# A linear-attention block gated by a mixer MLP: one more pair of feature chunks of the last block in seven products, one unused split less, and a new order

## The chip, the core and the metric

The kernel runs on one core of a Trainium2 chip. The metric is the device time of one execution in microseconds. The core has five engines that each work through a list of their own, in order: PE (TensorE, matrix products), DVE (VectorE), ACT (ScalarE), POOL (GpSimd) and SP (SyncE). In this kernel SP issues the plain transfers, and POOL issues the transfers that add to what stands at their destination. Engines wait for each other by semaphores only.

## The reference

The input `x` has 2048 tokens of 512 features. It is layer-normed, goes through a linear attention with 32 heads of 16 features, and the result is multiplied by a gate: a SiLU of a mixer block with an MLP of 1376 features.

```python
def _A_ref(x, wqkv, wo):
    q, k, v = ...                                  # x @ wqkv, 32 heads of 16
    phi = lambda t: jnp.where(t > 0, t + 1, jnp.exp(t)) + 1e-6
    pq, pk = phi(q), phi(k)
    kv = jnp.einsum("bhsd,bhse->bhde", pk, v)
    o = num / den                                  # pq @ kv over pq . sum(pk)
    return o @ wo
def _B_ref(x, w1, w2, w3, w4):
    h = _gelu(_layernorm(x) @ w1)
    x1 = x + shifted_by_quarters(h) @ w2           # shifts of +1, -1, +2, -2 tokens
    return x1 + _gelu(_layernorm(x1) @ w3) @ w4
xn = _layernorm(x)
return x + _A_ref(xn, ...) * _silu(_B_ref(xn, ...))
```

## The kernel before, in words

Tokens are worked in four blocks of 512 (four tiles of 128 each). Every fp32 operand of a product is split into a rounded high part and the rest (`halves`, `rounded`, `split`: one ACT or DVE copy and one DVE subtraction), and a product is three matmuls: high x high, low x high, high x low (`products`, L514). All matmuls are issued from L151.

First come keys, queries and the sums over tokens (`key`, `keys_queries`, `gram`) together with the first half of the mixer (`mix1`, tiles `h`; `mix2`, tiles `pam`, `pbm`, `pem`). Its weight `w1` is centred first: four chunks of `w1` are added by a load and three adding transfers of POOL into `w1t`, summed over rows by PE (`w1m`), scaled by ACT, and added to the four raw chunks `w_s` by four more transfers of POOL. Then the sums over tokens, `v`'s weight and `wo` are folded into one 512 x 512 matrix `M`, held as quarters `b11`, `b12`, `b21`, `b22` and four combinations `t1` to `t4`, each split in two.

Then the MLP runs block by block. Its 1376 features are 11 chunks of at most 128: five pairs (chunk s with chunk s + 5) and a last one of 96. `up_pair` (L1293) or `up_plain` (L1270) make a pair's hidden features; both take seven products of halves in place of eight (`seven`, L948, Strassen's scheme in Winograd's form). What comes back down is taken by `downs` (L1360) in one of two ways. For a pair whose number is below `SEVENS[b]` of its block, the down product is also made of seven products: `up_pair` forms four sums and differences of the hidden quarters (`s1` to `s4`), `make_t4` (L1183) or the memory `w4t` gives those of `w4` (`t1` to `t4`), five products stream into the accumulators (`STREAM`), and the other two (`s2 t2`, `s3 t3`) are done for all such pairs at the last of them, in `chain` (L1386), through the bank `uc`. For the other pairs and the last chunk, `plain` (L1353) makes the products of each token tile directly. `SEVENS` (L464) holds the number for each block.

The attention is done for two tiles at a time (`attend_pair`, tiles `pas`, `pbs`, `pes`, result `so`), and `gate` (L1481) finishes a token tile: it adds the accumulator to `e` (what `chain` and the residual left there), takes SiLU on ACT (`th`), multiplies by `so` on DVE, adds `x`, and stores. In the last block tiles 2 and 3 have `x` loaded ahead (`xr`, a DVE addition); tiles 0 and 1 add it by a transfer of POOL from memory (`pl.gather(th, x[rows])`), and the store follows it. The last half of tile 3 has its accumulator in the bank `a4x`, into which the residual `xi` goes by two matmuls. In the last block the down products of the last `keep` groups are left for the end, token tile by token tile (L1683 and the loop over `rest`).

The code doesn't run in the order in which it is written. Each operation is recorded, and `Plan.emit` (L296) lays the recorded list out in time with its own durations for every operation: of those that are ready on an engine it takes the one with the earliest due time. Due times come from a matmul's place in the written order, passed back to what it needs. `nudged` (L253) changes the due time of single operations by a table, `SOONER`: pairs of an operation's number and a step of a quarter microsecond by which it is due sooner (or later, with a minus). What comes out is one fixed list for each engine.

Of the kernel before, what the change touches and what calls it, by code (L numbers as in the profile page):

```python
# [27 lines left out]
class Tile:  # L28
# [16 lines left out]
    @property  # L45
    def all(self):
        return self[:, :]
# [383 lines left out]
def linear_attn_gated_by_mixer(  # L431
# [29 lines left out]
    EARLY = (), ()  # L461
    QAT, SAT = ((2, 3),) * 4, ((4, 5),) * 4
    HURRY = 3.0
    SEVENS = 0, 2, 3, 3  # L464
    FIRST7 = 1
    SUMS = "DVE"
    LATE = QT
# [16 lines left out]
    def piece(name, dt=F32):  # L484
        return pl.new("p", name, dt, PIECE)[:, :512]

    def rounds(name):

        return piece(name + "h", F32R), piece(name + "l", F32R)
# [13 lines left out]
    def both(pair, a, z):  # L503

        return tuple(v.cols(a, z) for v in pair)

    def in2(v, n=TH):

        return v.via(lambda ap: ap.rearrange("p (c n) -> p c n", n=n))
# [12 lines left out]
    def rounded(hi, lo, full, src=None):  # L522

        pl.act(hi, src or full, AF.Copy)
        split(lo, full, hi)

    def halves(name, src):

        hi, lo = rounds(name)
        rounded(in2(hi), in2(lo), src)  # L530
        return [both((hi, lo), c * TH, (c + 1) * TH) for c in range(2)]
# [688 lines left out]
    def load_group(b, s):  # L1220
# [4 lines left out]
        if s == "last":  # L1225
            load_w4(b, FB - 1)
            return
        if s >= SEVENS[b]:
            for f in (s, s + NS):
                load_w4(b, f)  # L1230
            return
        if all(s >= n for n in SEVENS[:b]):
            make_t4(b, s)
# [59 lines left out]
    def up_pair(b, s):  # L1293

        if s >= SEVENS[b]:
            up_plain(b, s)
# [63 lines left out]
    def downs(b, acc, s, which=range(QT)):  # L1360
        fs = (FB - 1,) if s == "last" else (s, s + NS)
        if b < FIRST7:
            for f in fs:
                for j in range(QT):
                    down(b, f, j, acc[j].all)
        elif s != "last" and s < SEVENS[b]:
            if s < SEVENS[b] - 1:
                stream(b, acc, s)
# [17 lines left out]
    def chain(b, n):  # L1386
# [3 lines left out]
        t, e = UC[b][0][0].tile, EV[b]  # L1390
        for s in range(SEVENS[b]) if n else ():
            x, y = CHAIN[n]
# [42 lines left out]
    def forms_m():  # L1435
        tf = [piece(f"m_f{k}") for k in range(4)]
        ts = right([in2(MQ[h][d]) for h in range(2) for d in range(2)], lambda k: in2(tf[k]))
        for k, v in enumerate(ts):
            M[f"t{k + 1}"] = halves(f"m_t{k + 1}", v)

# [22 lines left out]
    def attend_pair(i):  # L1463
# [3 lines left out]
        z = [o1.cols(0, TH), o1.cols(TH, 512), o2.cols(TH, 512), o2.cols(0, TH)]  # L1467
        ps = seven(f"s{i}", z, lambda x, y: [QF[i][x][c] + M[y][c] for c in range(2)])
        pl.act(z[3], ps, AF.Copy)
# [149 lines left out]
    b = NQ - 1  # L1619
# [24 lines left out]
    MQ = [[piece(f"mq{h}{d}") for d in range(2)] for h in range(2)]  # L1644
# [11 lines left out]
    for gg in range(NC):  # L1656
        ps = bank(f"m{gg}")
        products(ps, [both(kvs, gg * P, (gg + 1) * P) + wos[gg]])
        for d in range(2):
            pl.act(MQ[gg // 2][d].cols(gg % 2 * TH, (gg % 2 + 1) * TH), ps.cols(d * TH, (d + 1) * TH), AF.Copy)  # L1660
    M = {f"b{h + 1}{d + 1}": halves(f"m_b{h + 1}{d + 1}", in2(MQ[h][d])) for h in range(2) for d in range(2)}
    turn_y(0)
    load_last()
    load_group(0, "last")
# [1 line left out]
    for b in range(NQ):  # L1666
        last = b == NQ - 1
        acc = [pl.new("acc", f"acc{b}_{j}", F32, 512) for j in range(QT)] if b < FIRST7 else {}
        if b >= FIRST7:
            t = [pl.new("acc", f"a{j}_{b}", F32, 512) for j in range(QT)]  # L1670
            side = [[half(v, d) for d in range(2)] for v in t]
            if last:
                side[QT - 1][1] = half(pl.new("mm", "a4x", F32, 512), 0)
            for k, (h, d) in QUARTER.items():
                acc[k] = [(side[2 * h + j][d], d == 0 or last and h == j == 1) for j in range(2)]
            acc["rows"] = [[(v.all, 0, 512)] for v in t]
            if last:
                acc["rows"][QT - 1] = [(side[QT - 1][d], d * TH, (d + 1) * TH) for d in range(2)]
            t = pl.new("mm", f"uc{b}", F32, 512)
            acc["a1"] = UC[b] = [(half(t, j), j == 0) for j in range(2)]  # L1680
        n7 = SEVENS[b]
        groups = list(range(n7)) + ["last"] + list(range(n7, NS))
        keep = 3 if last else 2  # L1683
        for n, s in enumerate(groups):
            if b == 0 and 0 < n < NS:
                load_pair(n)
            if n < NS:
                load_group(b, groups[n + 1])
            elif not last:
                load_group(b + 1, 0 if SEVENS[b + 1] else "last")  # L1690
            if s == "last":
                up_last(b)
            else:
                up_pair(b, s)
            if b == 0 and n == 1:
                forms_m()
            if n > 0:
                for k in range(2):
                    if n == QAT[b][k]:
                        for j in range(2):  # L1700
                            turn_q(b * QT + 2 * k + j)
                        forms_q(b * QT + 2 * k)
            if n > 0 and n - 1 < len(groups) - keep:
                downs(b, acc, groups[n - 1])
            for k in range(2):
                if n == SAT[b][k]:
                    attend_pair(b * QT + 2 * k)
        rest = groups[len(groups) - keep:]

        if b < FIRST7:  # L1710
            turn_y(b + 1)
            for s in rest:
                downs(b, acc, s)
            for j in range(QT):
                gate_tile(b, j, acc[j].all)
        elif not last:
            turn_y(b + 1)
            for s in rest:
                downs(b, acc, s)
            for j in range(QT):  # L1720
                gate(b, j, acc["rows"][j][0][0])
        else:
            xr = {}
            for j in (2, 3):
                xr[j] = piece(f"xr{j}")
                pl.load(xr[j], x[(b * QT + j) * P:(b * QT + j + 1) * P, :])
            t = piece("xi", F32R)
            hi, lo = t.cols(0, TH), t.cols(TH, 512)
            rounded(hi, lo, EV[b][QT - 1].cols(TH, 512))
            pl.patience = 0.0  # L1730
            for j in range(QT - 1):
                for s in rest:
                    downs(b, acc, s, (j,))
                gate(b, j, acc["rows"][j][0][0], xr=xr.get(j))
            for r, a, z in acc["rows"][QT - 1]:
                if a:
                    for v in (hi, lo):
                        pl.mm(r, identr.all, v, False, False, more=True)
                for s in rest:
                    for f in (FB - 1,) if s == "last" else (s, s + NS):  # L1740
                        ah, al, n = H3[b, f]
                        left = both((ah.rows(n), al.rows(n)), (QT - 1) * P, QT * P)
                        products(r, [left + both(W4[b, f], a, z)], False, more=True)
                gate(b, QT - 1, r, a, TH, xr=xr[QT - 1], whole=a > 0)

    SOONER = (
# [16 lines left out]
    )  # L1763
    pl.emit(first=6.0, lead={"p": 14.0, "w": 14.0}, reserve={"p": 20, "w": 1}, window=12.0,
            ahead=6.0, table=SOONER)
# [37 lines left out]
```

## Time and profile before

| | |
|---|---|
| median of 3 runs | 502.06 us (501.93 to 503.35) |
| profiled execution, first to last instruction (span) | 501.2 us, 0.9 us under the median |
| PE | 494.3 us busy (99%), 3102 matmuls |
| DVE, ACT, POOL | 440.9 us (88%), 388.9 us (78%), 84.9 us (17%) |
| granted TensorE clock | 1.000 |

The profile's own span runs from the first to the last instruction of one execution; the run's time also holds what lies around it. A matmul of 512 columns stands with about 0.39 us in the list, and the next one starts 0.23 us after it: the records overlap, so that a busy PE says that work stood there, and the distance from start to start says how fast it went.

### The profile page before, as it was taken

The numbers are of one execution on the slowest core, as the hardware profiler recorded it, in microseconds if no ns is written. First come the engines' busy times: TensorE is split into PE (matmuls) and PEld (weight loads), VectorE is DVE, ScalarE is ACT, GpSimd is POOL, SyncE is SP. The second block draws the span as 40 slices with busy tenths as digits, with TensorE's granted clock in tenths as the row PEclk, the third lists the DMA queues.
The fourth block names the chain that finished last, engine by engine and source line by source line (L and its number), as shares of the span: only waits on it lengthen the run. The fifth ranks groups of instructions, "written<-read, shape, count | busy, mean of one in ns | idle before, by whom it ended". The sixth has DMA issues, their size and how long they took to land.

```text
span 501.2 us, 9464 instructions
## 1 busy us (share of the span) xinstructions
PE 494.3 (99%) x3102; PEld 442.2 (88%) x3102; DVE 440.9 (88%) x944; ACT 388.9 (78%) x859; POOL 84.9 (17%) x97
## 2 busy tenths in 40 slices
PE   8999999999999999999999999999999999999996
PEld 6777887898888888899999989999899998999986
DVE  5989999999699995999999998897799969998364
ACT  5999899867798884977777579957699878977551
POOL 1344433131221122020100002200020200201100
PEclk9999999999999999999999999999999999999999
DMA  7949985479994799979897599978699887898604
GB/s 245 365 110 239 319 261 144 106 149 269 322 260 134 191 336 233 262 198 286 266 319 243 193 312 260 269 235 245 190 252 305 225 192 239 278 314 266 154 8 120
DMA packets 86989, 116.69 MB, mean 233 GB/s; under 512 B 8864, under 2 KB 41148, under 8 KB 86940
## 3 DMA queue, kind: packets, MB, share of 16 engines
q1 hardware_dynamic: 77004, 98.00, 60.3%
q0 software_dynamic: 9936, 18.09, 20.9%
q8 instruction: 24, 0.39, 0.3%
q14 instruction: 25, 0.20, 0.2%
HBM read 73.70 MB, written 32.91 MB: 213 GB/s over the span
## 4 chain that ended last, share of the span: by engine, by line
PE 88%; DMA 8%; SPq 1%; ACT 1%; issue 0%; DVE 0%; POOL 0%; DVEq 0%
PE a L151 15%; PE pb L151 11%; PE h L151 9%; PE pbk L151 7%; PE g L151 7%; PE acc L151 6%; PE pe L151 6%; DMA w1t<-in_w 5%; PE pbm L151 5%; PE pbs L151 4%; PE uc L151 3%; PE pek L151 3%; PE pa L151 3%; PE pem L151 2%; PE pes L151 2%; PE pak L151 2%
## 5 line engine op out<-in xcount | busy, mean ns | idle before, releaser
L230 POOL DMA_DIRECT2D th<-in_x x14 | 12.3, 926 | 164.4 <-DMA w_t<-w4t 75.6
L230 POOL DMA_DIRECT2D o<-x x16 | 14.1, 895 | 65.1 <-DVE o L198 48.0
L178 ACT ACT_TABLE_LOAD x18 | 23.1, 1283 | 0.3
L652 POOL TENSOR_TENSOR rs<-w,nhalf 128x4 f32<-128x4 f32 (+2 forms) x10 | 16.7, 1675 | 38.1 <-DVE w L203 38.1
L173 ACT ACTIVATE gf<-gf 128x256 f32<-128x256 f32 (+1 forms) x48 | 22.0, 469 | 1.2 <-DVE gf L198 0.8
L230 POOL DMA_DIRECT2D zacc<-kr x16 | 16.4, 1022 | 36.5 <-DMA zacc<-kr 13.2
L230 POOL DMA_DIRECT2D e<-x1d x12 | 10.6, 1084 | 62.0 <-DVE e L198 44.1
L208 DVE SCALAR_TENSOR_TENSOR kr<-kt,kr 128x512 f32<-128x512 f32 x16 | 11.0, 686 | 4.4 <-ACT kt L173 4.4
L173 ACT ACT_TABLE_LOAD x11 | 14.1, 1283 | 1.0 <-PEq L1794 0.8
L173 ACT ACTIVATE ht<-ht 128x512 f32<-128x512 f32 x16 | 9.8, 623 | 6.5 <-DVE ht L198 6.5
L646 DVE BATCH_NORM_STATS2 st<-o 128x6 f32<-128x512 f32 x16 | 10.6, 681 | 4.7 <-DMA o<-x 4.7
L198 DVE TENSOR_TENSOR e<-a,e 128x512 f32<-128x512 f32 (+1 forms) x17 | 9.7, 587 | 5.1 <-PE a L151 5.1
L198 DVE TENSOR_TENSOR th<-th,so 128x512 f32<-128x512 f32 (+1 forms) x17 | 10.9, 648 | 3.3 <-ACT th L173 3.3
L173 ACT ACTIVATE x<-x,nm,rs 128x512 f32<-128x512 f32 x16 | 12.9, 805 | 0.0
L173 ACT ACTIVATE p<-pe 128x256 f32<-128x256 f32 x20 | 7.6, 382 | 6.7 <-PE pe L151 6.5
L173 ACT ACTIVATE p<-pb 128x256 f32<-128x256 f32 x20 | 7.6, 381 | 6.7 <-PE pb L151 6.5
L173 ACT ACTIVATE y<-o,nm,rs 128x512 f32<-128x512 f32 x16 | 11.8, 804 | 1.2 <-DVE nm L208 1.2
L173 ACT ACTIVATE th<-e 128x512 f32<-128x512 f32 (+1 forms) x12 | 7.1, 608 | 7.1 <-DVE e L198 7.1
L208 DVE SCALAR_TENSOR_TENSOR pq<-pq,qr 128x512 f32<-128x512 f32 x12 | 8.2, 686 | 3.9 <-ACT pq L173 3.8
L198 DVE TENSOR_TENSOR ht<-h,abc 128x512 f32<-128x512 f32 x16 | 10.8, 681 | 0.4 <-PE h L151 0.4
L198 DVE TENSOR_TENSOR gf<-pb,p 128x256 f32<-128x256 f32 x20 | 8.4, 418 | 3.1 <-PE pb L151 3.0
L208 DVE SCALAR_TENSOR_TENSOR qz<-pq,zb 128x512 f32<-128x512 f32 x16 | 10.7, 684 | 0.2
(1868 smaller groups left out, 2285.1 us busy)
## 6 DMA issues: line engine op xcount, KB each, us to landing
w_s<-in_w SPq DMA_DIRECT2D x34, 256.0 KB, 4.8
w_t<-w4t SPq DMA_DIRECT2D x26, 256.0 KB, 4.5
w_b<-w4d SPq DMA_DIRECT2D x24, 256.0 KB, 5.3
x<-in_x SPq DMA_DIRECT2D x16, 256.0 KB, 6.3
zacc<-kr POOLq DMA_DIRECT2D x16, 256.0 KB, 4.8
o<-x POOLq DMA_DIRECT2D x16, 256.0 KB, 4.7
x1d<-o SPq DMA_DIRECT2D x16, 256.0 KB, 3.8
xt<-in_xt SPq DMA_DIRECT2D x15, 256.0 KB, 6.2
```

What stands on the lines that cost most here:

```text
L151: lambda: nc.tensor.matmul(out.get(), lhs.get(), rhs.get(), start=start, stop=stop, skip_group_check=more))
L173: nc.scalar.activation(out.get(), src.get(), func, scale=get(scale), **kw)
L178: op.warm = lambda: nc.scalar.activation(self.scr[1].get(), self.scr[0].get(), func)
L198: self.vec(eng, out, [a, b], lambda: self.e(eng).tensor_tensor(out.get(), a.get(), b.get(), op=op), True)
L208: lambda: self.nc.vector.scalar_tensor_tensor(out.get(), a.get(), get(s), b.get(), op0=op0, op1=op1),
L230: lambda: self.nc.gpsimd.dma_start(out.get(), get(src), accum_op=ALU.add))
L646: pl.add("DVE", .62, .69, [xv], [st], lambda: nc.vector.bn_stats(st.get(), xv.get()))
L652: lambda: g.tensor_tensor(out.get(), src.get(), nh.get(), op=ALU.pow))
```

## The change

Three edits:

- `SEVENS` is `0, 2, 3, 4` in place of `0, 2, 3, 3`: in the last block pair 3 (chunks 3 and 8) takes seven down products too. `chain` now comes at pair 3, and `keep` is 2 for all blocks: the last chunk and pair 4 are left for the end, where the last chunk and the pairs 3 and 4 were.
- The quarter `b12` of the matrix `M` is no longer split into high and low part. None of the seven products uses it by itself.
- The table `SOONER` has another content: 1831 pairs in place of 163.

```diff
-    SEVENS = 0, 2, 3, 3
+    SEVENS = 0, 2, 3, 4
...
-    M = {f"b{h + 1}{d + 1}": halves(f"m_b{h + 1}{d + 1}", in2(MQ[h][d])) for h in range(2) for d in range(2)}
+    M = {f"b{h + 1}{d + 1}": halves(f"m_b{h + 1}{d + 1}", in2(MQ[h][d])) for h, d in ((0, 0), (1, 0), (1, 1))}
...
-        keep = 3 if last else 2
+        keep = 2
...
     SOONER = (
-        2, 309, 19, 38290, 23, 20, 24, 16, 26, 2469, 31, 130, 36, 38310, 42, 1201, 43, 154, 54, 5, 55, 36, 62, 32,
...
+        0, 800, 1, 227, 2, -732, 3, -637, 4, 627, 5, 416, 6, 55, 7, 1378, 8, -4, 9, -7, 10, 21, 11, -267, 12, -499,
...
+        5403, 22,
     )
```

The table moves instructions on every engine, from the first load to the last store. Three places follow; a row is line, operation, output tile, input tiles and size, with buffer numbers at the names' ends, and rows of an engine are executed in this order.

PE, the first block's mixer products `h`, from the first use of `w1`'s chunk 1 (`w_1h`) to the first use of chunk 2 (`w_2h`). Before, where six products with chunk 0 stand ahead of these rows:

```order
L151 MATMUL h_0_622<-u_1h,w_1h 128x512
L151 MATMUL h_0_622<-u_1l,w_1h 128x512
L151 MATMUL h_2_627<-u_1h,w_1h 128x512
L151 MATMUL h_0_622<-u_1h,w_1l 128x512
L151 MATMUL h_2_627<-u_1l,w_1h 128x512
L151 MATMUL h_2_627<-u_1h,w_1l 128x512
L151 MATMUL h_1_657<-u_0h,w_0h 128x512
L151 MATMUL h_1_657<-u_0l,w_0h 128x512
L151 MATMUL h_1_657<-u_0h,w_0l 128x512
L151 MATMUL h_1_657<-u_1h,w_1h 128x512
L151 MATMUL h_0_622<-u_2h,w_2h 128x512
```

Now, where eight products with chunk 0 stand ahead of these rows:

```order
L151 MATMUL h_0_634<-u_1h,w_1h 128x512
L151 MATMUL h_0_634<-u_1l,w_1h 128x512
L151 MATMUL h_1_647<-u_0h,w_0l 128x512
L151 MATMUL h_1_647<-u_1h,w_1h 128x512
L151 MATMUL h_0_634<-u_1h,w_1l 128x512
L151 MATMUL h_0_634<-u_2h,w_2h 128x512
```

The first use of chunk 2 was the 17th of these products and is the 14th.

PE, the third block's mixer: products of the token sums (`g`), of the mixer's first half (`h`) and the first of its second half (`pbm`, from the split hidden tile `ha112h`). Before:

```order
L151 MATMUL h_1_1935<-u_2h,w_2l 128x512
L151 MATMUL h_1_1935<-u_3h,w_3h 128x512
L151 MATMUL h_1_1935<-u_3l,w_3h 128x512
L151 MATMUL h_1_1935<-u_3h,w_3l 128x512
L151 MATMUL g_401<-k9l,x9h 128x512
L151 MATMUL g_401<-k9h,x9l 128x512
L151 MATMUL g_410<-k9h,x9h 128x512
L151 MATMUL g_410<-k9l,x9h 128x512
L151 MATMUL g_410<-k9h,x9l 128x512
L151 MATMUL pbm_2085<-w_b11h,ha112h 128x256
L151 MATMUL pbm_2085<-w_b11l,ha112h 128x256
```

Now:

```order
L151 MATMUL h_3_2033<-u_2h,w_2l 128x512
L151 MATMUL h_3_2033<-u_3h,w_3h 128x512
L151 MATMUL h_3_2033<-u_3l,w_3h 128x512
L151 MATMUL pbm_2071<-w_b11h,ha112h 128x256
L151 MATMUL h_3_2033<-u_3h,w_3l 128x512
L151 MATMUL g_369<-k8h,x8l 128x512
L151 MATMUL g_369<-k9h,x9h 128x512
```

The first `pbm` product stood after all `h` products of the block, with its fellows behind it; now it stands alone, ahead of the last `h` product.

The end of PE's list. `a_3` are the accumulators of the last block, `a4x` the one of the second half of tile 3, `pes` a bank of the attention of tiles 2 and 3. Before:

```order
L151 MATMUL a4x<-w_3_8h,f_8h 128x256
L151 MATMUL a4x<-w_3_8l,f_8h 128x256
L151 MATMUL a4x<-w_3_8h,f_8l 128x256
L151 MATMUL a4x<-w_3_4h,f_4h 128x256
L151 MATMUL a4x<-w_3_4l,f_4h 128x256
L151 MATMUL a4x<-w_3_4h,f_4l 128x256
L151 MATMUL a4x<-w_3_9h,f_9h 128x256
L151 MATMUL a4x<-w_3_9l,f_9h 128x256
L151 MATMUL a4x<-w_3_9h,f_9l 128x256
```

Now:

```order
L151 MATMUL a_3_6446<-w_3_9l,f_9h 128x512
L151 MATMUL a_3_6446<-w_3_9h,f_9l 128x512
L151 MATMUL a_3_6391<-w_3_4h,f_4l 128x512
L151 MATMUL a_3_6391<-w_3_9h,f_9h 128x512
L151 MATMUL a_3_6391<-w_3_9l,f_9h 128x512
L151 MATMUL a_3_6391<-w_3_9h,f_9l 128x512
L151 MATMUL pes_7122<-m_b22h,q14s1h 128x256
L151 MATMUL pes_7122<-m_b22l,q14s1h 128x256
L151 MATMUL pes_7122<-m_b22h,q14s1l 128x256
L151 MATMUL pes_7122<-m_b22h,q14s1h 128x256
L151 MATMUL pes_7122<-m_b22l,q14s1h 128x256
L151 MATMUL pes_7122<-m_b22h,q14s1l 128x256
```

And the end of DVE's list, the additions `e` and multiplications `th` of the last four token tiles. Before:

```order
L198 TENSOR_TENSOR e_6782<-a_3_6357,e_6782 128x512
L198 TENSOR_TENSOR th_0_7122<-th_0_7122,so_7080 128x512
L198 TENSOR_TENSOR e_6786<-a_3_6402,e_6786 128x256
L198 TENSOR_TENSOR th_0_7122<-th_0_7122,xr_6835 128x512
L198 TENSOR_TENSOR th_0_7142<-th_0_7142,so_7089 128x256
L198 TENSOR_TENSOR th_0_7142<-th_0_7142,xr_6857 128x256
L198 TENSOR_TENSOR th_256_7158<-th_256_7158,so_7089 128x256
L198 TENSOR_TENSOR th_256_7158<-th_256_7158,xr_6857 128x256
```

Now (`e_6774` and `th_0_7206` are tile 0, `e_6765` and `th_0_7188` tile 1, `th_0_7174` tile 2, `th_0_7155` half of tile 3):

```order
L198 TENSOR_TENSOR e_6765<-a_3_6446,e_6765 128x512
L198 TENSOR_TENSOR th_0_7155<-th_0_7155,so_7138 128x256
L198 TENSOR_TENSOR e_6774<-a_3_6391,e_6774 128x512
L198 TENSOR_TENSOR th_0_7188<-th_0_7188,so_6985 128x512
L198 TENSOR_TENSOR so_7125<-u2s_7073,pes_7122 128x256
L198 TENSOR_TENSOR th_0_7155<-th_0_7155,xr_6848 128x256
L198 TENSOR_TENSOR th_0_7174<-th_0_7174,so_7125 128x512
L198 TENSOR_TENSOR th_0_7174<-th_0_7174,xr_6837 128x512
L198 TENSOR_TENSOR th_0_7206<-th_0_7206,so_6949 128x512
```

The list ended with tile 3, whose `x` is in `xr`; it now ends with tile 0, whose `x` comes by a transfer of POOL. POOL's last two transfers are these additions of `x` in both kernels, for tiles 0 and 1 (`th_0_7048`, `th_0_7066` before, `th_0_7188`, `th_0_7206` now). SP's last stores were those of tiles 0, 1, 2 and the two halves of 3, and are now those of the halves of 3, then 2, 1 and 0.

193 rows, old and new, of the table SOONER are left out of this document.

## The prediction

> **What bounds the kernel now.** I read the page, then who PE waits for, then the start and the end in order of time. The page (busy time by engine, and the chain that ended last):
>
> ```profile
> span 501.2 us, 9464 instructions
> PE 494.3 (99%) x3102; PEld 442.2 (88%) x3102; DVE 440.9 (88%) x944; ACT 388.9 (78%) x859; POOL 84.9 (17%) x97
> PE 88%; DMA 8%; SPq 1%; ACT 1%; issue 0%; DVE 0%; POOL 0%; DVEq 0%
> ```
>
> All waits of PE in the whole execution (who for whom: us in total, times, longest):
>
> ```profile
> PE warm L151 <- POOL ones L548: 1.7, 1, 1.7
> PE w1m L151 <- ACT w1mh L173: 0.6, 1, 0.6
> PE h L151 <- ACT w_1h L173: 0.2, 1, 0.2
> ```
>
> So PE is the bound from the first product to its last matmul; behind the warm-up it waits 0.8 us by name. Time can change in three ways: fewer matmul columns, holes between matmuls, and what comes after the last matmul. Holes that no wait names show as wider steps (us, then busy and count by engine, clock, DMA share, GB/s):
>
> ```profile
> 5.50:12.00 6.50, 6.46 (x21) 4.27 (x22) 6.06 (x11) 3.81 (x7) 0.00 (x0) 1.00 1.01 314
> 32.10:46.00 13.90, 13.06 (x56) 9.65 (x56) 12.42 (x25) 12.97 (x36) 6.38 (x8) 1.00 0.81 173
> ```
>
> With the steps of 0.2325 us shown next, 21 wide matmuls take 4.9 of the first 6.5 us (1.6 lost), and of the second row's 56 (two are the narrow `ab` ones, hardly 0.03 us each) 12.6 of 13.9 us are used (1.3 lost). That is most of what PE can win back.
>
> **The change part by part: seven products.** The last matmuls of 512 and of 256 columns, first and last of five each:
>
> ```profile
> 491.83 0.40 PE L151 MATMUL a<-w_4l,f_4h 128*128 128x512 f32 x1
> 492.76 0.39 PE L151 MATMUL a<-w_9h,f_9l 128*128 128x512 f32 x1
> 496.20 0.28 PE L151 MATMUL a4x<-w_4l,f_4h 128*128 128x256 f32 x1
> 496.67 0.28 PE L151 MATMUL a4x<-w_9h,f_9l 128*128 128x256 f32 x1
> ```
>
> Four steps are 0.93 and 0.47 us: 0.2325 and 0.1175 us a matmul. Taken plainly, pair 3 costs 2 chunks x 3 tiles x 3 = 18 matmuls of 512 columns and, as tile 3 is done in halves, 12 of 256. In seven products it is 7 x 2 x 3 = 42 of 256. So 18 wide ones go and 30 narrow ones come: 30 x 0.1175 - 18 x 0.2325 = **-0.66 us**.
>
> The forms for it (DVE gets 12 more instructions, ACT 6, SP 7 transfers, with the two chunks of `w4` loaded again, four parts of `w4t` stored and read back) are made while PE works on the last block:
>
> ```profile
> 440.00:460.00 20.00, 20.00 (x171) 20.00 (x171) 16.96 (x40) 15.58 (x37) 0.86 (x1) 1.00 0.97 298
> 460.00:480.00 20.00, 20.00 (x162) 19.61 (x161) 10.45 (x24) 11.12 (x31) 3.51 (x4) 1.00 0.58 143
> ```
>
> Twelve DVE instructions of 0.42 to 0.69 us are at most 8 us; DVE is idle for 12.6 of these 40 us, ACT for 13.3. I take 0; without that cover PE stands still for what is late (a rival below). The split of `b12` that goes is one ACT and one DVE instruction where PE waits for neither: 0.
>
> **The order at the start.** The chunks of `w1` arrive by four POOL transfers:
>
> ```profile
> L230 POOL DMA_DIRECT2D w_s<-w1t x4: 909/1374/1894, 35.9 to 37.6; - x4
> DMA to landing us min/median/max: 3.4/6.4/8.6
> 44.80 0.49 PE L151 MATMUL h<-u_1h,w_1h 128*128 128x512 f32 x1 [0.22 <-ACT w_1h L173]
> 46.49 0.62 ACT L173 ACTIVATE w_2h<-w_s 128x512 fp32r<-128x512 f32 x1
> 46.55 0.39 PE L151 MATMUL h<-u_0l,w_0h 128*128 128x512 f32 x1
> 47.24 0.43 PE L151 MATMUL h<-u_2h,w_2h 128*128 128x512 f32 x1
> ```
>
> The last one, chunk 2, is issued at 37.6 and lands 8.6 us on, at 46.2; with its rounding on ACT (0.62) and two hand-overs of about 0.04 it can be used from 46.9. Before, its first use is the 17th `h` product, at 47.24, just not late. Now it is the 14th, and PE takes its list in order: the 14th product stood at 46.55 before (the row above) and can't start before 46.9 now. The two holes ahead of it, at `w1m` and `w_1h`, may close (their products stand later), but the wait for chunk 2 takes that back: **+0.35 us**. If all transfers of this chain come 1 us earlier, it is -0.65; 1 us later, +1.35.
>
> **The order in the middle.** Where `pbm` now stands alone, the first mixer tile must be ready 12 rows (2.8 us) after its last `h` product. Before:
>
> ```profile
> L173 ACT ACTIVATE ha112h<-ht x2: 400/408/417, 148.3 to 151.1; 128x256 fp32r<-128x256 f32 x2
> 154.78 0.28 PE L151 MATMUL pbm<-w_b11h,ha112h 128*128 128x256 f32 x1
> ```
>
> It was written at 151.5 and used at 154.78, 3.3 us later. Now DVE (0.69), GELU on ACT (0.63) and the rounding (0.41), with hand-overs about 2.0 us, must fit into 2.8: 0.8 us are left for what stands ahead on ACT, and two more 512-wide copies there (0.52 us a step) already make a hole. The new order strews single matmuls between other groups at many places, and behind the token sums only one narrow matmul instead of six covers the copy for `kv`. I bound the lot from -0.8 us (every named wait of PE gone) to +2.8 (six holes like those named, 0.2 to 0.6 each), and take **+1.0 us**: nearer to the cost, since there is little left to win and cover shrinks at the places I looked at.
>
> **The order at the end.** Let T be the end of the last matmul's record. Before, T = 496.67 + 0.28 = 496.95 and SiLU, two DVE steps and the store follow:
>
> ```profile
> 496.98 0.38 ACT L173 ACTIVATE th<-a4x 128x256 f32<-128x256 f32 x1 [0.92 <-PE a4x L151]
> 497.40 0.42 DVE L198 TENSOR_TENSOR th<-th,so 128x256 f32<-128x256 f32 x1 [0.40 <-ACT th L173]
> 497.86 0.42 DVE L198 TENSOR_TENSOR th<-th,xr 128x256 f32<-128x256 f32 x1
> 498.31 0.33 SPq L222 DMA_DIRECT2D out<-th  x1
> ```
>
> The store is issued at 498.31 and the span ends at 501.17, 2.86 us on: T + 4.2. What tiles 0 and 1 cost, which now come last (additions on DVE, SiLU; POOL's transfer and the store behind it, twice):
>
> ```profile
> 493.19 0.69 DVE L198 TENSOR_TENSOR e<-a,e 128x512 f32<-128x512 f32 x1 [1.67 <-PE a L151]
> 493.92 0.63 ACT L173 ACTIVATE th<-e 128x512 f32<-128x512 f32 x1 [1.74 <-DVE e L198]
> 494.58 0.69 DVE L198 TENSOR_TENSOR th<-th,so 128x512 f32<-128x512 f32 x1 [0.70 <-ACT th L173]
> 495.19 0.42 DVE L198 TENSOR_TENSOR e<-a,e 128x256 f32<-128x256 f32 x1
> 495.53 0.68 DVE L198 TENSOR_TENSOR th<-th,xr 128x512 f32<-128x512 f32 x1
> 486.62 0.86 POOL L230 DMA_DIRECT2D th<-in_x  x1 [20.30 <-issue]
> 489.51 0.86 POOL L230 DMA_DIRECT2D th<-in_x  x1 [2.02 <-DVE th L198]
> DMA to landing us min/median/max: 4.1/4.1/4.1
> 493.66 0.36 SPq L222 DMA_DIRECT2D out<-th  x1
> ```
>
> DVE starts follow each other by 0.61 (512 wide) or 0.34 us (256 wide), and a step that needs the one before waits for its end. Tile 0's last matmul ends six narrow ones before T, at T - 0.7. Its addition (0.69) runs to T + 0.0, its SiLU to T + 0.7. But its multiplication is the last of DVE's list, behind tile 1's multiplication (T - 0.1), the attention's `so` (T + 0.55), an `xr` addition (T + 0.9), tile 2's multiplication (T + 1.25) and the `xr` addition that needs it (T + 1.95): it starts at T + 2.55 and ends at T + 3.25. Then POOL's transfer, 4.1 us to landing, and the store, 2.86 us to the end: with hand-overs T + 10.3. Against T + 4.2 that is **+6.1 us**. Below: if POOL's transfer lands as fast as the store issued at 493.66, +4.0; that store's row in the view of `out` is:
>
> ```profile
> DMA to landing us min/median/max: 2.0/2.0/2.0
> ```
>
> Above: the two transfers, 2.6 us apart, hinder each other by 1 us, +7.1.
>
> For such a transfer the Trainium skill, page "DMA: Bandwidth & Descriptors", section "Anatomy of one DMA — SWDGE (gpsimd) path", gives a fit of about 2.0 us plus the bytes at 436 GB/s; for 256 KB that is an estimate of 2.6 us. The trace has 4.1 at both places, which I use; by the fit the time forecast would be 1.5 us lower, 507.3.
>
> **Sum**: 501.17 - 0.66 + 0.35 + 1.0 + 6.1 = 507.96 us of span. The median lies 0.89 above this execution's span, so 508.8 us.
>
> **Rivals.**
> - *PE runs so full that it pays for the end* (the other side: not slower). Place: the start. The 1.6 + 1.3 us of wide steps above close, and so do some 1.4 us elsewhere. T is then 0.66 + 4.3 us earlier, at 492.0, and the end is 6.1 longer: 501.17 - 4.96 + 6.1 + 0.89 = 503.2, no change that a measurement tells. It decides from a T of 492.4 on. For it: the `w1m` products stand later, so that their hole can close. Against: the wait for chunk 2, which pins PE at 46.9 whatever is won ahead of it.
> - *The last transfer is quick* (2.0 us, as the store). 508.8 - 2.1 = 506.7. The fit above points this way; both rows with 4.1 were taken in a quiet stretch, so little speaks for it.
> - *The forms of pair 3 are late.* Its `w4` is loaded, combined, stored, and two forms are read back: four transfers and two rounds of DVE and ACT, some 20 us, within the last 60 us. PE would wait in `uc` or `a`. A wait of 2 to 5 us gives 511 to 514. For it: DMA share 0.97 at 440 to 460. Against: 0.58 behind it, and idle engines.
> - *The end is not what I read*, and only the saving shows: 501.4. The lists are fixed, so that tile 0's chain would have to be shorter than each of its rows; hardly.
>
> **How the numbers follow.** Forecast 0.70; late forms 0.12; quick transfer 0.09; full PE 0.06; saving alone 0.03. The likeliest: 508.8 us. Its own bounds: end 4.0 to 7.1, middle -0.8 to +2.8, start -0.65 to +1.35; not all at once, so 505.7 to 511.2, which leaves out most of the late forms and of the full PE. A measurement tells about 0.3% (1.5 us) from no change. Slower by more: the first three cases, 0.91. Within: most of the full PE and half of the saving alone, 0.06. Faster: 0.03.
>
> **What would show it.** Seven products: 3120 matmuls, 18 fewer with 512 columns. Start: a wait of PE for `w_2h` of 0.3 to 1 us in place of those for `w1mh` and `w_1h`. Middle: new waits of PE for ACT around `pbm` and `kv`. End: the last PE instruction `pes`, some 10 us ahead of the span's end, POOL's last `th` about 3.3 us behind it and the last store 4.1 us behind that. I am wrong if the last matmul stands less than 8 us ahead of the end, or ends ahead of 494.5, or if PE waits for a form of pair 3 by more than 1 us.

## The result and the profile after

The changed kernel takes 511.11 us (median; 510.50 to 512.30) against 502.06 us: 9.05 us more, a ratio of 1.0177, 95% interval 1.0161 to 1.0193. The forecast was 508.8 us, its range 505.7 to 511.2: slower as forecast, 2.3 us more than that, and 0.1 us inside the upper end of the range. The page of the changed kernel (span; busy time by engine; the chain that ended last):

```profile
span 509.1 us, 9558 instructions
PE 493.9 (97%) x3114; PEld 441.7 (87%) x3114; DVE 446.6 (88%) x956; ACT 393.0 (77%) x865; POOL 86.8 (17%) x97
PE 73%; issue 13%; DMA 5%; ACT 3%; DVE 3%; POOL 1%; SPq 0%; POOLq 0%; DVEq 0%; ACTq 0%
```

PE is busy for 0.4 us less than before in a span that is 7.9 us longer. So the loss is time in which PE has nothing to do. The mean granted clock fell too, from 1.000 to 0.992, but that is no cause: in the windows view it is 1.00 up to PE's last matmul in both kernels and 0.60 only behind it, in the changed one. PE's waits in the changed kernel (who for whom: us in total, times, longest):

```profile
PE warm L151 <- POOL ones L548: 1.1, 1, 1.1
PE k L151 <- ACT u_0h L173: 1.0, 1, 1.0
PE pbm L151 <- ACT p1m L173: 0.7, 1, 0.7
PE h L151 <- ACT w_2h L173: 0.5, 1, 0.5
PE pbk L151 <- DVE p5k L198: 0.4, 1, 0.4
PE pbm L151 <- ACT ha112h L173: 0.4, 1, 0.4
PE pb L151 <- DVE gf L198: 0.3, 1, 0.3
```

Behind the warm-up they make 3.3 us, against 0.8 before. The other part stands at the end. The rows of the timeline there (start and duration in us, engine, line; in brackets the idle time before and who ended it):

```profile
497.54 0.69 DVE L198 TENSOR_TENSOR e<-a,e 128x512 f32<-128x512 f32 x1
497.92 0.27 PE L151 MATMUL pes<-m_b22h,q14s1l 128*128 128x256 f32 x1
498.26 0.63 ACT L173 ACTIVATE th<-e 128x512 f32<-128x512 f32 x1 [0.30 <-DVE e L198]
500.74 0.68 DVE L198 TENSOR_TENSOR th<-th,so 128x512 f32<-128x512 f32 x1
501.72 0.86 POOL L230 DMA_DIRECT2D th<-in_x  x1 [1.73 <-DVE th L198]
505.80 0.33 SPq L222 DMA_DIRECT2D out<-th  x1
```

T, the end of the last matmul's record, is 497.92 + 0.27 = 498.19 (496.95 before), and the span ends at 509.07: the tail behind T is 10.9 us, 4.2 before. Of the 7.9 us of span 6.65 are tail and 1.25 are T.

To see where T comes from I add up PE's lost steps: for each matmul the time to the next one's start, less the median step of its shape, where that is over 0.03 us. In before and after that is: up to 60 us 5.84 and 5.87; from 60 to 140 us 0.40 and 0.39; from 140 to 250 us **0.60 and 2.75**; from 250 to 354 us 0.41 and 0.40; behind that 0.46 and 0.86. PE's first matmul stands at 1.06 in place of 1.67, which gives 0.61 us back. With 0.66 us less to do this comes to +1.3 us, T's 1.25.

### The profile page after: what moved, and what is told of

Same layout as the page of the kernel before. It is cut to its first block, busy times and chain, and to the rows that moved or that the text cites. A ratio compares the mean times of both kernels' runs of the same rounds, so it can differ in the third digit from the quotient of the medians.

```text
span 509.1 us, 9558 instructions
## 1 busy us (share of the span) xinstructions
PE 493.9 (97%) x3114; PEld 441.7 (87%) x3114; DVE 446.6 (88%) x956; ACT 393.0 (77%) x865; POOL 86.8 (17%) x97
## 4 chain that ended last, share of the span: by engine, by line
PE 73%; issue 13%; DMA 5%; ACT 3%; DVE 3%; POOL 1%; SPq 0%; POOLq 0%; DVEq 0%; ACTq 0%
PE a L151 10%; PE pb L151 8%; PE g L151 6%; PE h L151 6%; PE acc L151 6%; PE pbk L151 6%; PE pbm L151 4%; PE pe L151 4%; PE pbs L151 3%; PE pek L151 3%; PE k L151 2%; PE pem L151 2%; PE uc L151 2%; PE pa L151 2%; PE pes L151 2%
## 5 line engine op out<-in xcount | busy, mean ns | idle before, releaser
L652 POOL TENSOR_TENSOR rs<-w,nhalf 128x4 f32<-128x4 f32 (+2 forms) x10 | 18.0, 1796 | 46.1 <-DVE w L203 46.1
L173 ACT ACTIVATE u<-pb 128x256 f32<-128x256 f32 x20 | 7.6, 379 | 5.5 <-PE pb L151 5.4
L198 DVE TENSOR_TENSOR ht<-h,abc 128x512 f32<-128x512 f32 x16 | 10.8, 680 | 1.2 <-PE h L151 1.2
L208 DVE SCALAR_TENSOR_TENSOR qz<-pq,zb 128x512 f32<-128x512 f32 x16 | 10.9, 684 | 0.2
L173 ACT ACTIVATE e<-uc 128x256 f32<-128x256 f32 x24 | 7.8, 380 | 4.0 <-PE uc L151 3.1
L198 DVE TENSOR_TENSOR th<-th,so 128x512 f32<-128x512 f32 (+1 forms) x17 | 10.8, 648 | 0.1
L208 DVE SCALAR_TENSOR_TENSOR pq<-pq,rd 128x512 f32<-128x512 f32 x16 | 10.8, 675 | 0.0
```

The source lines that it names most:

```text
L173: nc.scalar.activation(out.get(), src.get(), func, scale=get(scale), **kw)
L198: self.vec(eng, out, [a, b], lambda: self.e(eng).tensor_tensor(out.get(), a.get(), b.get(), op=op), True)
L208: lambda: self.nc.vector.scalar_tensor_tensor(out.get(), a.get(), get(s), b.get(), op0=op0, op1=op1),
L652: lambda: g.tensor_tensor(out.get(), src.get(), nh.get(), op=ALU.pow))
```

## Experiments

To undo the new order in parts, the planner gets a list of operations in the order in which it has to issue them, and chooses nothing as long as that list lasts:

```diff
+        given = [ops[n] for n in reversed(given)]
...
+            pick = given.pop() if given else None
             for e, cands in avail.items():
+                if pick:
+                    cands = [pick] if pick in cands else []
```

The list is made of the two kernels' orders. The buffers' rotation and the waits follow from it.

### The old order with seven products, and three kernels that go over to the new order ever later

```diff
+    GIVEN = old order up to 385 us; behind it sorted anew, tile 3 last
```

> Seven products for pair 3 and no split of b12, as in the change, but every engine keeps the order it had before, up to about 385 us; behind that the products, forms and transfers of the last block are sorted anew so that the second half of tile 3 ends last, as before. Ledger theory (saving 0.66 us, all the rest of the loss is order): T, the end of the last matmul, 0.66 us earlier than before, tail T + 4.2, so 502.06 - 0.66 = 501.4 us. Rival 'forms of pair 3 late': PE waits for w4 or f forms of pair 3 for 1 us or more, 502.5 us or slower. Rival 'the split that went was needed' (something waits for it): a named wait behind 200 us, also slower than before.

Measured: 501.89 us, ratio 0.9990 (0.9981 to 1.0000). Span and busy times on its page:

```profile
span 500.3 us, 9526 instructions
PE 493.2 (99%) x3114; PEld 441.4 (88%) x3114; DVE 445.7 (89%) x956; ACT 390.8 (78%) x864; POOL 84.8 (17%) x97
```

The last matmul and the last store in its timeline:

```profile
495.62 0.28 PE L151 MATMUL a4x<-w_9h,f_9l 128*128 128x256 f32 x1
497.26 0.33 SPq L222 DMA_DIRECT2D out<-th  x1
```

T is 495.90, the tail 4.4. The same 3114 matmuls as in the changed kernel, the same forms of pair 3, the same split left out, and no loss at all: the nine microseconds are in the order alone. PE waits for no form of pair 3 here, nor in the changed kernel, so the rival of late forms falls; the time alone could not have told it, since 511.11 us lies in its 511 to 514 as well. The kernel is 0.5 us slower than the 501.4 expected; part of that is its own newly sorted end, with a tail of 4.4 us in place of 4.2.

```diff
+    GIVEN = old order up to 85 us, then the changed kernel's
```

> The changed kernel, with the order of before for what is issued in the first 85 us alone (the h products with chunk 2 of w1 stand where they stood). Ledger theory, with the start mis-sized by no more than its bounds: PE's wait for w_2h goes, 0.3 to 0.9 us are won against the changed kernel: 510.2 to 510.8 us. Rival 'the start costs nothing, all is in the middle and the end': 511.1 us, same as the changed kernel within 0.2.

Measured: 510.56 us, ratio 1.0166 (1.0145 to 1.0186), T = 498.07. The wait for `w_2h` is gone. The time is 0.55 us less than the changed kernel's, as the ledger had it, but the executions of both overlap and T is only 0.1 us earlier: the price of the start is not shown by this run.

```diff
+    GIVEN = old order up to 354 us, then the changed kernel's
```

> The changed kernel, with the order of before for what is issued in the first 354 us (start and the three blocks up to there); the rest of the last block and the end in the new order. Ledger theory: beside the start, the holes at pbm, kv and pbk between 140 and 240 us close, about 1.7 us more than the kernel that keeps only the first 85 us: 508.5 to 509.1 us, T close to the one of before less 0.1. Rival 'the middle holes only take the place of others' (PE is bound by DVE or ACT there and waits elsewhere): less than 0.5 us more than the other, about 510.3.

Measured: 509.42 us, ratio 1.0136 (1.0118 to 1.0154): 1.1 us less than with the old order up to 85 us, not the 1.7 expected, and the executions of the two overlap. In the profiled execution, one of the faster ones (508.39 us), T is 495.51, 2.6 us earlier than there. The windows view shows what has closed: from 140 to 250 us PE issues 635 matmuls here and 617 in the changed kernel (window, its length, busy us and count of PE, PEld, DVE, ACT, POOL, then clock, DMA share, GB/s; this kernel, then the changed one):

```profile
140.00:250.00 110.00, 110.00 (x635) 96.10 (x634) 101.16 (x219) 88.65 (x189) 18.16 (x21) 1.00 0.85 239
```

```profile
140.00:250.00 110.00, 108.63 (x617) 93.75 (x616) 98.96 (x215) 83.25 (x177) 18.09 (x21) 1.00 0.91 259
```

The lost steps in this stretch are 0.31 us here and 2.15 with the old order up to 85 us. So the rival that the waits only change places falls by the traces: with the old order all engines get more done in this stretch. How much of it reaches the time, 1 us or 2, the runs leave open.

```diff
+    GIVEN = old order up to 488 us, then the changed kernel's
```

> Old order for all that is issued before 488 us, new order for the last 8 us of PE alone: tiles 0 and 1 end last, their x is added by POOL's transfer. Ledger theory: T 0.66 us earlier than before, tail 10.9 us as in the changed kernel, against 4.2: 502.06 - 0.66 + 6.7 = 508.1 us. Rival 'the end is cheap and the new order costs on PE': near 503. Against old_order_seven the difference is the price of the end alone, 6.7 us by the trace of the changed kernel, 6.1 as forecast.

Measured: 508.83 us, ratio 1.0134 (1.0116 to 1.0152). Its page has a span of 507.0 us; the last matmul and the last store in its timeline:

```profile
495.07 0.28 PE L151 MATMUL pes<-m_b22h,q14s1l 128*128 128x256 f32 x1
503.71 0.33 SPq L222 DMA_DIRECT2D out<-th  x1
```

T = 495.35 is the best of the four, the tail 11.6. The kernel takes 0.7 us more than the 508.1 expected, as much as the tail is longer. The last 8 us of PE in the new order cost 508.83 - 501.89 = 6.9 us against the first kernel of this ladder: the end is the largest term by far.

### The new order with the old end

```diff
+    GIVEN = the changed kernel's order up to 470 us; behind it sorted anew, tile 3 last
```

> The changed kernel in the new order up to about 470 us; only the last 25 us are sorted so that tiles 0 and 1 end early (their x by POOL well before the end) and the second half of tile 3 ends last, as in the kernel before. Ledger theory: T as in the changed kernel (498.2 in its profile), the tail 4.2 to 4.4 us in place of 10.9: 6.5 us less than the changed kernel, 504.3 to 504.8 us. Rival 'the holes on PE make most of the loss': 508 us or more.

Measured: 505.48 us, ratio 1.0068 (1.0053 to 1.0084). The span is 502.5 us; the last matmul and the last store in the timeline:

```profile
497.49 0.28 PE L151 MATMUL a4x<-w_9h,f_9l 128*128 128x256 f32 x1
499.25 0.40 SPq L222 DMA_DIRECT2D out<-th  x1
```

T = 497.76, tail 4.7, in an execution that was the fastest of six (504.40 us). The median is 5.6 us less than the changed kernel's and 0.7 us above what I expected, 0.3 to 0.5 us of it in the tail. The loss that stays, 3.2 us against the 502.28 us of the kernel before beside it, belongs to PE's holes (T is 1.9 to 2.7 us later than in the two executions with the old order and this end) and to the time outside the span. Both halves of the ledger are there without each other.

### Tile 0's multiplication first

```diff
 TENSOR_TENSOR e<-a,e 128x512
 TENSOR_TENSOR th<-th,so 128x512
+TENSOR_TENSOR th<-th,so 128x512
 TENSOR_TENSOR so<-u2s,pes 128x256
 TENSOR_TENSOR th<-th,xr 128x256
 TENSOR_TENSOR th<-th,so 128x512
 TENSOR_TENSOR th<-th,xr 128x512
-TENSOR_TENSOR th<-th,so 128x512
```

> The changed kernel; in DVE's list alone the multiplication of tile 0 moves ahead of the attention's so, the xr additions and the multiplication of tile 2, and POOL's transfer follows it. Ledger theory: the multiplication ends at T + 1.4 in place of T + 3.25, so the tail is 1.8 us shorter: 509.3 us. Rival 'the two transfers of POOL, now under 1 us apart, hinder each other' (upper bound of the end in the prediction): the second lands 5 us or more behind its issue, and no more than 0.9 us is won: 510.2 us.

Measured: 513.60 us, ratio 1.0221 (1.0195 to 1.0247). Nothing is won. The last matmul, the moved multiplication, POOL's two transfers and the last store in the timeline:

```profile
500.23 0.27 PE L151 MATMUL pes<-m_b22h,q14s1l 128*128 128x256 f32 x1
501.23 0.69 DVE L198 TENSOR_TENSOR th<-th,so 128x512 f32<-128x512 f32 x1
501.43 0.86 POOL L230 DMA_DIRECT2D th<-in_x  x1 [20.39 <-DVE th L198]
502.22 0.96 POOL L230 DMA_DIRECT2D th<-in_x  x1
508.02 0.33 SPq L222 DMA_DIRECT2D out<-th  x1
```

The landing of the two, in the view of the instructions that write `th`, POOL's alone:

```profile
DMA to landing us min/median/max: 3.8/4.8/5.8
```

The multiplication ends at T + 1.4 as planned and the second transfer is issued at T + 1.7 in place of T + 3.5. But it takes 5.8 us in place of 4.1, lands at T + 7.5 as before, and the tail is 10.8. The rival holds, and more than it said: the whole 1.8 us goes into the second transfer. T itself, 500.50, is 2.3 us later than in the changed kernel, though the lists up to there are the same. So the same kernel once more:

> The kernel of mult_first once more. Its lists are those of the changed kernel up to the last ten instructions of DVE, ACT and POOL, and its tail behind T was the same, yet its median was 2.5 us above the changed kernel's. Theory 'chance of the executions': 510.5 to 512 us now, as the changed kernel and pbm_back. Rival 'something in this kernel is slower': 513 us or more again.

Measured: 510.55 us, ratio 1.0161 (1.0144 to 1.0178); T = 497.65, the second transfer 5.7 us to landing, tail 10.7. The tail is the same as before, so that reading stands. T is not: it moves with the execution, by more than the terms that I call the start.

### x of tiles 0 and 1 loaded ahead

```diff
-            for j in (2, 3):
+            for j in range(QT):
                 xr[j] = piece(f"xr{j}")
```

> The changed kernel; x of tiles 0 and 1 is loaded ahead, at about 478 us, and added on DVE in the place in which POOL's transfer stood, so that the last transfers of POOL go. Two loads and two DVE additions (0.68 us each) come, two POOL transfers go. Ledger theory: the transfer (4.06 us and 0.3 ahead of it) was on the path, an addition of 0.68 takes its place and pushes the multiplication by 0.6: 3.0 us less, 508.1 us. Rival 'the last store ends late whatever stands ahead of it' or 'the transfers were covered': less than 1 us won, 510 us or more.

Measured: 507.70 us, ratio 1.0115 (1.0101 to 1.0130). The last matmul, the last addition and the last store in the timeline (span 505.6 us):

```profile
497.60 0.28 PE L151 MATMUL pes<-m_b22h,q14s1l 128*128 128x256 f32 x1
501.74 0.69 DVE L198 TENSOR_TENSOR th<-th,xr 128x512 f32<-128x512 f32 x1
502.45 0.33 SPq L222 DMA_DIRECT2D out<-th  x1
```

3.4 us are won, and the tail is 505.62 - 497.88 = 7.7 us. What stands on the path now is DVE's list: its last addition ends at T + 4.55, and the store follows at once.

### One POOL transfer in place of two

```diff
-            for j in (2, 3):
+            for j in (1, 2, 3):
```

> As mult_first (tile 0's multiplication ahead of the rest of DVE's list), but x of tile 1 is loaded ahead and added on DVE, so that POOL has one transfer left, tile 0's, with nothing of its own queue beside it. Theory 'the pair hinders each other' (from mult_first, where the second transfer took 5.8 us to landing in place of 4.1): the lone transfer lands 3.8 to 4.1 us behind its issue, the tail is T + 9.0 in place of 10.8, 1.8 us less than the changed kernel, 509.3 us. Rival 'the stores to out of the same microseconds slow it': it lands 5 us or more behind its issue, tail 10.3 or more, 510.7 us.

Measured: 509.65 us, ratio 1.0142 (1.0125 to 1.0160). The same rows of the timeline as for the pair (span 508.2 us):

```profile
498.20 0.28 PE L151 MATMUL pes<-m_b22h,q14s1l 128*128 128x256 f32 x1
499.20 0.69 DVE L198 TENSOR_TENSOR th<-th,so 128x512 f32<-128x512 f32 x1
500.43 0.86 POOL L230 DMA_DIRECT2D th<-in_x  x1 [21.42 <-issue]
504.87 0.33 SPq L222 DMA_DIRECT2D out<-th  x1
```

And the landing in the view of POOL's writes to `th`:

```profile
DMA to landing us min/median/max: 4.4/4.4/4.4
```

Without the other transfer in its queue the last one lands 4.4 us behind its issue, not 5.8: the pair hinders itself. The packet records of POOL's queue in the traces say how. The lone transfer's 144 packets begin 1.6 us behind its issue and run from 501.99 to 504.45. In the run with the pair 288 run on end from 503.02 to 507.65. Counted off, the second transfer's 144 begin at 504.81, 2.6 us behind its issue: it waits about 1 us for the first's, and then takes 2.8 us in place of 2.5. It does not take the 3.8 to 4.1 us that I expected either, and POOL issues it 0.54 us behind the end of the multiplication. So the tail is 9.7 in place of 9.0, 1.2 us shorter than the changed kernel's. Whether the stores beside it account for the 0.3 us was not tried.

### Two single instructions in the middle

```diff
 MATMUL h<-u_3l,w_3h 128x512
-MATMUL pbm<-w_b11h,ha112h 128x256
 MATMUL h<-u_3h,w_3l 128x512
...
 MATMUL g<-k9h,x9h 128x512
+MATMUL pbm<-w_b11h,ha112h 128x256
 MATMUL pbm<-w_b11l,ha112h 128x256
```

> The changed kernel with one matmul moved on PE: the pbm that stands alone among the products near 151 us goes back behind them, beside the other five of its group. Theory of the forecast (the lone pbm loses its cover and makes a hole of its own): the step of 0.51 us ahead of it goes, T and the time are 0.5 us less, 510.6 us. Rival 'the hole is set by what ACT and DVE have ready': the same 0.5 us is lost within the next 40 us and the time stays at 511.1 us.

Measured: 510.58 us, ratio 1.0175 (1.0161 to 1.0188). The wait has gone from `pbm` and stands five microseconds later in this kernel's timeline:

```profile
156.74 0.38 PE L151 MATMUL pem<-w_t1h,hs12h 128*128 128x256 f32 x1 [0.42 <-ACT hs12h L173]
```

The lost steps from 140 to 160 us are 1.28 us in place of 0.86, those from 140 to 250 us 2.43 in place of 2.75. The time is 0.5 us less than the changed kernel's, as the theory had it, but the executions of both overlap, and the lost steps side with the rival. The lone `pbm` was only the first matmul that met the lack; my reason for this hole falls. What is late is ACT. In the timeline of the changed kernel the middle of block 3's mixer reads

```profile
145.97 1.30 DVE L198 TENSOR_TENSOR ht<-h,abc 128x512 f32<-128x512 f32 x2
147.33 1.28 ACT L173 ACT_TABLE_LOAD   x1 [0.74 <-issue]
148.97 0.68 DVE L198 TENSOR_TENSOR ht<-h,abc 128x512 f32<-128x512 f32 x1
150.72 0.62 ACT L173 ACTIVATE ht<-ht 128x512 f32<-128x512 f32 x1
151.54 0.40 ACT L173 ACTIVATE ha112h<-ht 128x256 fp32r<-128x256 f32 x1
152.00 0.38 PE L151 MATMUL pbm<-w_b11h,ha112h 128*128 128x256 f32 x1 [0.35 <-ACT ha112h L173]
```

and in that of the kernel before

```profile
142.27 0.69 DVE L198 TENSOR_TENSOR ht<-h,abc 128x512 f32<-128x512 f32 x1 [0.22 <-PE h L151]
142.65 1.28 ACT L173 ACT_TABLE_LOAD   x1
```

DVE takes up the first tile of `h` products 3.7 us earlier there, and ACT loads GELU's table (1.28 us) ahead of the four `y` copies. Now ACT does the copies first, stands idle for 0.74 us and loads the table 4.7 us later, and all that the mixer needs comes behind that: the tile that `pbm` waits for leaves DVE at 149.65, its GELU starts 1.07 us later, and another rounding stands between GELU and its own. This is read from the two traces; to bring the tile forward alone was not tried.

```diff
 ACTIVATE k14h<-kr 128x512
+ACTIVATE p1m<-pbm 128x256
 ACTIVATE x14h<-x 128x512
 ACTIVATE w_1_s1h<-w_1_sf 128x512
-ACTIVATE p1m<-pbm 128x256
```

> The changed kernel with one instruction moved in ACT's list near 180 us: the copy p1m<-pbm, for which PE waited 0.7 us there, goes ahead of the roundings x14h and w_s1h. Theory of the forecast (each hole of the middle is a place with too little cover, and can be closed by itself): the wait of PE for p1m goes, the time is 0.5 to 0.8 us less, 510.4 us. Rival 'the middle holes are one shortage of ACT and DVE that shows wherever PE comes next' (as pbm_back, where the hole only moved 5 us on): the excess of PE's steps from 140 to 250 us stays between 2.0 and 2.8 us and the time at 510.5 to 511.2 us.

Measured: 511.61 us (510.29 to 512.88), ratio 1.0193 (1.0167 to 1.0220). In its timeline the copy is early and PE's next group comes without a wait:

```profile
180.21 0.38 ACT L173 ACTIVATE p1m<-pbm 128x256 f32<-128x256 f32 x1 [1.29 <-PE pbm L151]
181.06 0.28 PE L151 MATMUL pbm<-w_t2h,hs22h 128*128 128x256 f32 x1
```

Its lost steps from 140 to 250 us are 1.75, 1.0 less than in the changed kernel, and T is 0.7 us earlier. But the time of the kernel is no less. This hole is open in some executions of the new order only (from 180 to 200 us 1.6 and 1.8 us lost in two, 0.1 to 0.8 in the others), so the run tells neither theory for good.

### The saving, once more

> The kernel of old_order_seven once more, to size the saving of the seven products better: 0.66 us less than before by the ledger (ratio 0.9987); its first comparison gave 0.999 with an interval of 0.9981 to 1.0. Rival 'the new forms take the saving back': ratio 1.0.

Measured: 501.50 us, ratio 0.9993 (0.9982 to 1.0005); T = 495.07. The two comparisons put the seven products at 0.3 us (from medians of 502.21 to 501.89 and of 501.77 to 501.50), and both intervals hold the 0.66 us of the forecast as well. This kernel beats the changed one by 9.2 us (511.11 less the 501.89 of its first comparison). That it beats the one before is not shown: one interval ends at 1.0000, the other holds 1.

## Why the prediction was right, and where its sum fell short

The direction, the place of each loss and the end step by step were right. That the time lies in the range owes something to luck: four terms were too small (middle, PE behind 250 us, end, outside the span), all on the same side, and only 0.1 us was left to the upper end. The executions profiled let me fill in the ledger with medians: five with the old order in the middle (lost steps from 140 to 250 us 0.30 to 0.60, median 0.33) and nine with the new one (1.59 to 3.86, median 2.33). The start is the first matmul's time and the lost steps up to 60 us, 7.4 us in the new order and 7.0 in the old; the tail is 10.8 us with the new end and 4.4 with the old. The row of the seven products holds the forecast's count in all columns; what the kernels with the old order gained in time is 0.3 us.

| term | forecast | before and after | medians over the profiles |
|---|---|---|---|
| seven products | -0.66 | -0.66 | -0.66 |
| start, to 60 us, with the earlier first matmul | +0.35 | -0.6 | +0.4 |
| middle, 60 to 250 us | +1.0 | +2.1 | +2.0 |
| PE behind 250 us | 0 | +0.4 | +0.6 |
| end | +6.1 | +6.65 | +6.4 |
| outside the span | 0 | not told | +0.3 |
| sum | +6.8 | +7.9 | +9.0 |

- **Seven products and split**: the count of wide matmuls fell by 18 and that of narrow ones rose by 30, as worked out; the total in "What would show it", 3120, was an error of addition (3102 + 12 = 3114). Costed at nothing for the forms: right, no wait for one of them.
- **Start**: size about right, by another way. The wait for chunk 2 came, as these rows of the changed kernel's timeline show, but so did one at the first `k` product; behind them POOL's loads of `w1` in the view of what writes `w_s` (duration in ns, first and last start in us):

```profile
5.82 0.74 PE L151 MATMUL k<-wk_0h,u_0h 128*128 128x512 f32 x2 [0.97 <-ACT u_0h L173]
45.82 0.50 PE L151 MATMUL h<-u_2h,w_2h 128*128 128x512 f32 x1 [0.53 <-ACT w_2h L173]
```

```profile
L230 POOL DMA_DIRECT2D w_s<-w1t x4: 857/1374/1896, 35.1 to 36.7; - x4
```

  Chunk 2 was usable at 45.8, not 46.9, since POOL issued it 0.9 us earlier; PE stood at its 14th product at 45.1. The two holes ahead of it did close. That the sum of these is near +0.35 is luck: in the two executions compared it is -0.6. The first 12 us, which I had not looked at in the new order, lose 4.4 to 5.6 us of steps against 3.6 to 4.1 with the old one, of which 0.6 is given back by the earlier first matmul.
- **Middle**: the step "take +1.0 us: nearer to the cost" was too small; the term is 2.0 by lost steps (1.1 by the times of the kernels with the old order up to 85 and 354 us). Its bounds were not well founded: -0.8 is made of waits that stand at the start, and six holes of up to 0.6 us are 3.6, not 2.8; one execution lost 3.5 us more than the old order's median. Signs and places were right (`pbm`, `ha112h`, ACT), the cause was only partly: not the lone matmul lost its cover, but ACT and DVE deliver later, and the copy of `pbm` that frees it for the next group stands behind two roundings on ACT. That ACT's late table load is behind all of it is read, not tested. The wait at `kv` that I expected is not among the named ones of the changed kernel; in three later profiles of the new order it is, at 0.2 us.
- **PE behind 250 us**: costed at nothing. It is 0.4 to 0.6 us. In the changed kernel it is one place, a product at 385 us that waits for DVE's `gf` (its step 0.47 us too wide); in other executions it is elsewhere, in the first one with tile 0's multiplication moved 0.41 us at 418 us, behind a load of `w4`.
- **End**: step by step as forecast: tile 0's addition at T - 0.66, its multiplication at T + 2.54 and POOL's transfer 4.06 us to landing. Too small were the hand-over from DVE to POOL (0.30 in place of 0.04; the trace of the kernel before has 0.54 and 0.29 at its two transfers, which the sum left out) and the last store (505.80 to 509.07, 3.27 in place of 2.86, which was that of a store half as large): 10.9 against 10.3. The rival of a quick transfer, toward which the Trainium skill's fit pointed (page "DMA: Bandwidth & Descriptors", section "Anatomy of one DMA — SWDGE (gpsimd) path"; an estimate of 2.6 us by it), falls: 3.7 to 5.8 us for all such transfers behind 480 us in the profiles here.
- **Outside the span**: I took the difference of median and span from one execution. Every later run lists both: the kernel before needs 1.7 us beside its span and the changed one 2.0, so that the execution profiled before was some 0.8 us slower than the median, and 0.3 us of the change is outside: 7.9 + 0.8 + 0.3 is the 9.0 measured. What does it is open.
- **PE pays for the end**: falls; T is later, not 4 us earlier.

## What to carry to other kernels

Before an order is taken over, follow each output's last chain behind the last matmul: a queue that puts the slowest way out last costs its whole length, here ten times the 0.66 us that the products were counted to save. An order found elsewhere should be costed where its slack is thin, with the spread of several executions in hand: the same lists lost 1.6 to 3.9 us in one stretch. And look for the engine that is late rather than for the matmul that meets the lack.

## What the runs showed of the hardware

- Two POOL transfers of 256 KB that add onto a tile, issued 0.8 us apart, land 2.8 us apart (3.8 and 5.8 us behind their issue; 3.7 and 5.7 in the second run). Issued 2.6 us apart they took 4.55 and 4.06 us (changed kernel), 2.0 us apart 3.9 and 3.8 (old order with seven products, first execution). To start the second earlier by 1.8 us brought nothing.
- From the end of the DVE multiplication to POOL's issue of the transfer that waits for it: of the 25 such transfers behind 480 us in the profiles, 0.30 us in 17 and 0.54 in 8. What decides between the two is open.
- A last store of 256 KB ends the span 3.2 to 3.3 us behind its issue in ten profiles here, one of 128 KB 2.9 to 3.2 in four.
- T, the end of PE's work, of one and the same list was 500.50 in one execution and 497.65 in another.
